# Attention and gated feed-forward on one core: another order inside the planned bursts of a head pair, and the turn of the row maxima as a matmul of its own

## The chip, the core and the metric

The kernel runs on one core of a Trainium2 chip. The metric is the device time of one execution in microseconds, lower is better. The core has a matmul engine (TensorE, "PE" in the profile; "PEld" is its loading of stationary operands), a vector engine (VectorE, "DVE"), an activation engine (ScalarE, "ACT"), a general engine (GpSimd, "POOL"), and SyncE ("SP"), which here only issues transfers. Matmuls write to the PSUM memory, from which only DVE and ACT read here. The kernel cuts PSUM into six single banks (`ps`) and a double one (`pv`). Each engine works through its own list of instructions in order.

## What is computed

Eight batches of eight heads, 576 positions, 64 features per head. Scores get a bias from cumulative sums, a causal mask and a softmax; then comes a feed-forward part with a convolution of three taps along the sequence and a sigmoid gate:

```python
scores = scale * np.matmul(q, k.transpose(0, 1, 3, 2))
cum = np.cumsum(np.maximum(s, 0.0), axis=-1)
bias = -(cum[:, :, :, None] - cum[:, :, None, :])
scores = np.where(causal, -1000000000.0, scores + np.minimum(bias, 0.0))
scores = scores - np.max(scores, axis=-1, keepdims=True)
attn = np.exp(scores)
attn = attn / (np.sum(attn, axis=-1, keepdims=True) + 1e-09)
x = np.matmul(attn, v)          # heads of a batch side by side: 512 features
h = np.maximum(x @ w_in, 0.0)   # 1024 features
conv_out = sum(conv_w[k] * hp[:, k:k + S, :] for k in range(3))
out = (h * (1.0 / (1.0 + np.exp(-conv_out)))) @ w_out
```

## The kernel before

**Pairs.** The 64 heads are worked on as 32 pairs, the two heads of a pair on the two halves of the partitions; four pairs make a batch. For each pair p the function `pair` lays down these steps, named as in the profile by their lines:

- Loads: q and k (L662), values (L667), rows for the bias (L688). Each number of q and k is split into a rounded part (L674) and a rest (L678, POOL).
- *Maxima parts* sh0 to sh3 (L719, PE): rough scores with queries on the partitions, from the rounded parts and the bias rows, two passes each. A part has two PSUM banks, one for each head of the pair. Parts 0 and 1 have 288 columns, parts 2 and 3 have 512 in two pieces each. DVE takes the maximum of each piece (L734) into a column of the tile `r8` and so frees the banks. `r8` has ten columns, five row tiles for each of two heads.
- *The turn* tn (L750, PE): the ten columns of maxima are transposed into rows in a PSUM bank; ACT copies them (L757), and SP moves them by two transfers into the tile `eq` (L763), from where they enter the scores.
- *Scores parts* sc0 to sc3 (L795, PE): the exact scores with keys on the partitions, three passes over q and k and one over bias rows and maxima. Again two banks a part, parts 0 and 1 of 288 columns, parts 2 and 3 of 512. ACT reads them through its exponential-like function (L810) into the tiles `pt` and frees the banks; POOL masks the diagonal blocks (L823).
- *Sums* (L865, PE): row sums of `pt` by a 32-column stationary operand, into one bank. DVE adds a guard and inverts (L884, L885); SP stores the result to memory (L890) and reads it back spread over the partitions (L899).
- *Values* pv (L847, PE): `pt` times the values, into the one double bank `pv`. DVE multiplies it by the inverse (L907, the step nm), ACT and DVE or POOL split the product for the feed-forward (L921, L925).

**Feed-forward.** For each batch and half of the sequence: `moe_h` makes the eight blocks of hidden features, 12 matmuls each (L956), with ReLU (L968) and center tap (L980) mostly on ACT, the two other taps on DVE (L994), the gate on ACT (L1007), the product on DVE (L1013), and the split into `u` (L1020, L1024). `moe_o` makes the four blocks of the output, 24 matmuls each in four chunks of six (L1050), which ACT or DVE copies (L1063) and SP stores. These matmuls use the full 128*128 array; sums use 128*32, values 128*64, scores and maxima 64*128, as the profile shows behind each operation.

**The plan.** Nothing is emitted in the order of the Python loops. Each step is a task with an engine, an estimated cost, the tasks it needs, a due time (tag) and the buffers it takes. `Sched.play` runs them through a simple model of the five engines and emits every engine's list in the order found. For PE it takes the ready task with the lowest tag, where a task in the same array mode as the one before counts as 8 us earlier (`STAY`). Modes are "r" for scores and maxima, "c32" for sums, "c" for values, and none for the feed-forward.

**Groups.** From pair 8 on (`B0`), matmuls of neighbouring pairs are tied into a group: once PE has begun a group, only tasks of this group (`burst`) are taken until it is finished. Group n holds the turn of pair n, the sums and values of pair n-1, the maxima parts of pair n+1 and the scores of pair n. Their order is written out in `ORDER`, and `link` makes it binding: each member follows the one before, and what the members need (handed over by `note`) must be done before the first of them:

```python
ORDER = ("tn", "sum", "pv", "sh0", "sh1", "sc0", "sh2", "sc1", "sh3", "sc2", "sc3")
for t, needs in seq:
    for d in needs:
        sch.need(d, first)
for (a, _), (c, _) in zip(seq, seq[1:]):
    sch.follow(a, c)
```

So the due time of the first member decides when a group competes with the feed-forward. The turn of pair p is due at `a_sh + 1` with `a_sh = at(p-1) + 0.05`, where `at` advances 20.5 us a pair; a maxima part of pair p+1, which stands in the same group, is due at `at(p) + 0.05`. Buffers around the change: `r8`, `rt` and `s` two of each, `ek` and `eq` three, `pt` three (two for a pair), `pv` and `rb` one, PSUM banks six.

Of the kernel before, what the change touches and what calls it, by code (L numbers as in the profile page):

```python
# [11 lines left out]
F32 = mybir.dt.float32  # L12
# [21 lines left out]
STAY = 8.0  # L34

B0 = 8
ORDER = ("tn", "sum", "pv", "sh0", "sh1", "sc0", "sh2", "sc1", "sh3", "sc2", "sc3")

# [39 lines left out]
class Sched:  # L80
# [4 lines left out]
    def add(self, name, opts, deps, tag, emit, alloc=(), uses=(), mode=None, nbytes=0, prev=None,  # L85
            burst=None):

        t = Task()
        t.name, t.opts, t.tag, t.emit = name, opts, tag, emit
        t.alloc, t.uses, t.mode, t.nbytes = alloc, list(alloc) + list(uses), mode, nbytes  # L90
        t.succ, t.start, t.seq, t.eng, t.done = [], None, len(self.tasks), None, None
        for b in t.uses:
            b.users += 1
        t.wait = 0
        for d in deps:
            if d is not None:
                d.succ.append(t)
                t.wait += 1
        t.then, t.burst = [], burst
        if burst is not None:  # L100
            self.size[burst] += 1
        if prev is not None:
            self.follow(prev, t)
        self.tasks.append(t)
        return t
# [142 lines left out]
def kernel(  # L248
# [10 lines left out]
    nc = tc.nc  # L259
    NP, P, _, S = qk.shape  # L260
# [11 lines left out]
    NT = (S + P - 1) // P  # L272
# [7 lines left out]
    const = ctx.enter_context(tc.tile_pool(name="const", bufs=1))  # L280
# [10 lines left out]
    ident = const.tile([P, P], F32, name="ident")  # L291
# [17 lines left out]
    PT_t = [const.tile([P, O_T[-1] + W_T[-1]], F32, name=f"pt{i}") for i in range(NPT)]  # L309
    X_t = const.tile([P, sum(NX), 2, XW], F32R, name="x")  # L310
    rb_t = const.tile([P, S], F32, name="rb")
    R8_t = [const.tile([P, 2 * NT], F32, name=f"r{i}") for i in range(2)]
    RT_t = [const.tile([2 * NT, P], F32R, name=f"rt{i}") for i in range(2)]
    rs_t = const.tile([P, RS], F32, name="rs")
    ri_t = const.tile([P, RS], F32, name="ri")
# [36 lines left out]
    def buf(name, n=1):  # L352
        return Buf(pools[name], n)

    def psb():
        return Buf(pool_ps)

    def bank(b, c0, c1):
        return ps_t[b.slot][:, c0:c1]
# [4 lines left out]
    def c_tt(n):  # L364
        return 0.155 + n / 0.96e3
# [4 lines left out]
    def c_pool(n):  # L370
        return 0.19 + n * 2.1e-3
# [21 lines left out]
    def c_ident(e):  # L393
        make_identity(nc, ident)

        nc.gpsimd.memset(mask, 0.0)
        nc.gpsimd.affine_select(
            out=mask[:, S - P : S], in_=mask[:, S - P : S], pattern=[[-1, P]],
            compare_op=ALU.is_ge, fill=NEG, base=0, channel_multiplier=1,
        )  # L400


        for pt in PT_t:
            nc.gpsimd.memset(pt[J_T[NT - 1] : P, O_T[NT - 1] :], 0.0)
        nc.gpsimd.memset(onehot, 0.0)
        for j in range(2):
            nc.gpsimd.memset(onehot[:, j, j : j + 1], 1.0)
# [10 lines left out]
    def c_ind(t):  # L418
# [9 lines left out]
        for i in range(NE)  # L428
    ]
    t_ident = add("ident", [("POOL", 2.5)], [], -189.5, c_ident)  # L430
    t_eb = add("eb", [("ACT", 0.72)], [t_masks], -188, c_ind(EB_t))
    t_ind = [
# [190 lines left out]
    def group(n, _=None):  # L623
        return n if n >= B0 else None

    def note(n, key, t, needs):
        if n >= B0:
            groups[n][key] = t, needs

    def link():  # L630
        for n, g in sorted(groups.items()):
            seq = [g[k] for k in ORDER if k in g]
            inside = {t for t, _ in seq}
# [4 lines left out]
            for (a, _), (c, _) in zip(seq, seq[1:]):  # L638
                sch.follow(a, c)

    last_ek, last_v = [None], [None]


    L = NT - 1
# [5 lines left out]
    def c_rt(n):  # L650

        return n * 0.461e-3

    def pair(p):
# [21 lines left out]
        def lo(e):  # L676
# [5 lines left out]
        t_lo = add(f"lo{p}", [("POOL", c_pool(2 * S), True), ("DVE", c_tt(2 * S), True, 4.0)],  # L682
                   [t_hi], A - 6, lo, uses=[raw, sb])
# [16 lines left out]
        r8, rt = buf("r8"), buf("rt")  # L700
        maxima = []
        t_mm = None
        for i, part in enumerate(SH_PARTS):
            pbs = [psb(), psb()]

            def sh_mm(e, part=part, pbs=pbs):
                o = 0
                for tau, c0, c1 in part:
                    dst = [bank(pb, o, o + c1 - c0) for pb in pbs]
                    qs = slice(P * tau, P * tau + P)  # L710
                    for k in range(2):
# [13 lines left out]
                       uses=[sb, ek], mode="r", prev=None if p - 1 >= B0 else t_mm,  # L725
                       burst=group(p - 1, f"sh{i}"))
            note(p - 1, f"sh{i}", t_mm, [t_hi, t_dr])
            for j in range(2):
                o = 0
                for tau, c0, c1 in part:  # L730
                    def sh_max(e, j=j, tau=tau, c0=c0, c1=c1, o=o, pb=pbs[j]):
# [12 lines left out]
                            sh_max, uses=[pbs[j], r8])  # L744
                    )
                    o += c1 - c0
        tb = psb()

        def turn(e):
            nc.tensor.transpose(bank(tb, 0, P)[0 : 2 * NT, :], R8_t[r8.slot], ident)  # L750

        t_turn = add(f"tn{p}", [("PE", 0.13)], maxima + [t_ident], a_sh + 1, turn, alloc=[tb, rt],
                     uses=[r8], mode="c32", burst=group(p))
        note(p, "tn", t_turn, maxima)

        def rt_cp(e):
            copy_on(e)(RT_t[rt.slot], bank(tb, 0, P)[0 : 2 * NT, :])  # L757
# [3 lines left out]
        def d_shift(e):  # L761
            for j in range(2):
# [6 lines left out]
        t_shift = add(f"ds{p}", [("SP", 1.5)], [t_rt, *t_ind], a_sh + 1, d_shift, alloc=[eq],  # L769
                      uses=[rt], nbytes=30000)  # L770
# [4 lines left out]
        t_sc = None  # L775
        for i, part in enumerate(SC_PARTS):
            pbs = [psb(), psb()]

            def sc_mm(e, part=part, pbs=pbs):
                o = 0  # L780
                for t, c0, c1 in part:
                    i0, cn = P * t + c0, c1 - c0
                    ks = slice(P * t, P * t + P)
                    dst = [bank(pb, o, o + cn) for pb in pbs]
                    st = S_t[sb.slot].rearrange("p a c -> p (a c)")
                    for k in range(4):
                        for j, r in enumerate(lanes):
                            if k < 3:
                                kk, kq = ((2, 3), (0, 3), (2, 1))[k]
                                l = st[r, kk * S + P * t : kk * S + P * t + P]  # L790
                                m = st[r, kq * S + i0 : kq * S + i0 + cn]
                            else:
                                l = EK_t[ek.slot][r, ks]
                                m = EQ_t[eq.slot][r, PAD + i0 : PAD + i0 + cn]
                            nc.tensor.matmul(dst[j], l, m, start=(k == 0), stop=(k == 3))  # L795
                    o += cn

            w = sum(c1 - c0 for _, c0, c1 in part)
            t_sc = add(f"sc{p}.{i}", [("PE", 4 * c_rt(w))], [t_shift, t_lo], A + 0.1 * i,
                       sc_mm, alloc=pbs + (pts if i == 0 else []), uses=[sb, ek, eq], mode="r",  # L800
                       prev=None if p >= B0 else t_sc, burst=group(p))
            note(p, f"sc{i}", t_sc, [t_lo])
            for j in range(2):
                o = 0
                for t, c0, c1 in part:
                    w = c1 - c0

                    def sc_exp(e, j=j, t=t, c0=c0, c1=c1, o=o, pb=pbs[j]):
                        jt = J_T[t]
                        nc.scalar.activation(  # L810
                            PT_t[pts[j].slot][0:jt, O_T[t] + c0 : O_T[t] + c1],
                            bank(pb, o, o + c1 - c0)[0:jt], AF.Sigmoid,
                            bias=bias_sb[0:jt, t, 2 * p + j : 2 * p + j + 1], scale=0.125,
                        )

                    t_exp = add(f"ex{p}.{j}.{t}.{c0}", [("ACT", 0.25 + w / 1.2e3)],
                                [t_sc, t_bias] + (t_bx if p < 2 else []), A + 0.1 * i, sc_exp,
                                uses=[pbs[j], pts[j]])

                    def sc_mask(e, j=j, t=t):  # L820
                        jt, dg = J_T[t], min(P, W_T[t])
                        reg = PT_t[pts[j].slot][0:jt, O_T[t] : O_T[t] + dg]
                        nc.gpsimd.affine_select(  # L823
                            out=reg, in_=reg, pattern=[[1, dg]], compare_op=ALU.is_ge, fill=0.0,
                            base=0, channel_multiplier=-1,
                        )

                    if c0 == 0:
                        t_exp = add(f"mk{p}.{j}.{t}", [("POOL", 0.29, True)], [t_exp],
                                    A + 0.1 * i, sc_mask, uses=[pts[j]])  # L830
                    masks.append((t, t_exp))
                    o += w


        pv, sb_ = buf("pv"), psb()
# [19 lines left out]
        def sums(e):  # L855

            for t in range(NT):
                for j in range(2):
# [17 lines left out]
        t_pv = add(f"pv{p}", [("PE", 2.75)], [t_v] + [m for t, m in masks], tq + 0.1,  # L876
                   pv_mm(range(NT)), alloc=[pv], uses=[vb, *pts], mode="c",
                   prev=None if p + 1 >= B0 else t_sum, burst=group(p + 1))
        note(p + 1, "sum", t_sum, [t_v] + [m for t, m in masks])
        note(p + 1, "pv", t_pv, [])  # L880
        ri, rb = buf("ri"), buf("rb")

        def inverse(e):
# [23 lines left out]
            nc.vector.tensor_tensor(rb_t, pvt[:, PV0 : PV0 + S], rb_t, op=ALU.mult)  # L907

        t_norm = add(f"nm{p}", [("DVE", 0.77)], [t_rb, t_pv], tq, norm, uses=[rb, pv])
        x = [buf("x0"), buf("x1")]  # L910
        x_bufs[p] = x

# [10 lines left out]
        def x_lo(e):  # L923
# [6 lines left out]
                        tq, x_lo, uses=[rb, *x])  # L930
# [144 lines left out]
    for p in range(NP):  # L1075
        pair(p)
# [63 lines left out]
```

## Time and profile before

| | us |
|---|---|
| three executions | 891.0, 898.09, 901.85 |
| median | 898.09 |
| profiled execution | 900.18 |
| its span, first to last instruction | 898.3 |
| mean granted TensorE clock in it | 0.95 |

The profile belongs to one execution. Its rows count from the first instruction. A timeline row gives start, duration, engine, line, operation, what is written and read, and the number of instructions merged; in brackets stands the idle time of the engine before it and what ended it. A group row gives busy time and the mean duration of one in ns, then the idle time of the engine before these instructions, by cause. Matmuls overlap: the duration of one is longer than its distance to the next, so lengths are best taken from start to start.

### The profile page before, as it was taken

How to read it: one execution, taken by the hardware profiler on the slowest of the kernel's cores; microseconds unless marked ns; L12 is line 12 of the kernel's file. 1: busy time of each engine (PE TensorE's matmuls, PEld its weight loads, DVE VectorE, ACT ScalarE, POOL GpSimd, SP SyncE). 2: the span in 40 equal slices, each digit the busy share in tenths (PEclk: the TensorE clock that was granted, in tenths of full speed). 3: DMA queues.
4: the chain of work that ended last, by engine and by line, in shares of the span. 5: the costliest groups of instructions: out<-in, count | busy, mean ns of one | idle time of the engine just before them, and what ended most of it. 6: DMA issues, size and time to landing. Idle time of an engine off the chain costs nothing.

```text
span 898.3 us, 20425 instructions
## 1 busy us (share of the span) xinstructions
PE 816.2 (91%) x7973; PEld 726.2 (81%) x7973; DVE 554.8 (62%) x1400; ACT 432.9 (48%) x958; POOL 328.6 (37%) x484
## 2 busy tenths in 40 slices
PE   2868688888999999999999999999899999999997
PEld 1746567778888889988888879888788888989996
DVE  8676877884757663766648563766537664636441
ACT  3445454644546363635536263635436363645541
POOL 7334444453332343333523343333423243222211
PEclk9988687896999999999999999999999999999998
DMA  6343323322121222122221222122212211110000
GB/s 183 125 122 110 107 84 107 108 78 89 48 82 60 81 65 65 52 81 67 67 66 49 80 66 69 48 80 68 58 57 66 80 41 29 32 47 17 25 28 26
DMA packets 50187, 63.20 MB, mean 70 GB/s; under 512 B 6063, under 2 KB 39151, under 8 KB 50031
## 3 DMA queue, kind: packets, MB, share of 16 engines
q1 hardware_dynamic: 50091, 61.91, 23.0%
q8 instruction: 62, 1.02, 0.5%
q14 instruction: 34, 0.28, 0.1%
HBM read 48.60 MB, written 13.04 MB: 69 GB/s over the span
## 4 chain that ended last, share of the span: by engine, by line
PE 68%; DVE 10%; DMA 9%; issue 2%; SPq 2%; ACT 1%; POOLq 0%; DVEq 0%; ACTq 0%
PE ps L956 23%; PE ps L1050 22%; PE pv L847 8%; PE ps L795 7%; PE ps L865 6%; DMA rb<-ri_d 6%; DVE junk L734 4%; PE ps L719 3%; DMA ri_d<-ri 2%; DVE rb L907 2%; DMA ht<-w_out 1%; SPq L899 1%; DVE ct L994 1%; DVE ri L885 1%; DVE ct L546 0%
## 5 line engine op out<-in xcount | busy, mean ns | idle before, releaser
L810 ACT ACTIVATE pt<-ps,bias_sb 128x288 f32<-128x288 f32 (+4 forms) x384 | 157.2, 480 | 156.7 <-PE ps L795 129.8
L1050 PE MATMUL ps<-u,wo 128*128 128x288 f32 x1536 | 221.4, 301 | 5.9 <-POOL u L1024 2.9
L956 PE MATMUL ps<-x,wi 128*128 128x290 f32 x1536 | 224.4, 304 | 1.1 <-ACT pt L810 1.0
L1050 PEld LDWEIGHTS ps<-u,wo 128*128 128x128 f32 x1536 | 212.3, 192 | 9.1 <-POOL u L1024 4.1
L956 PEld LDWEIGHTS ps<-x,wi 128*128 128x128 f32 x1536 | 215.8, 195 | 3.4 <-ACT pt L810 1.6
L994 DVE SCALAR_TENSOR_TENSOR ct<-ht,cw_sb,ct 128x288 f32<-128x288 f32 (+1 forms) x256 | 143.6, 564 | 101.3 <-ACT ct L980 96.7
L823 POOL TENSOR_SCALAR_AFFINE_SELECT pt<-pt 128x128 f32<-128x128 f32 x320 | 97.4, 321 | 249.1 <-ACT pt L810 241.5
L1024 POOL TENSOR_TENSOR u<-ct,u 128x576 fp32r<-128x576 f32 x64 | 96.5, 1508 | 225.0 <-ACT u L1020 187.3
L734 DVE CUSTOM_DVE_ANT_0 junk<-ps,mask 128x320 bf16<-128x320 f32 (+2 forms) x320 | 137.5, 430 | 61.2 <-PE ps L719 35.8
L795 PE MATMUL ps<-s 64*128 64x288 f32 (+4 forms) x1152 | 141.5, 334 | 29.8 <-DVE r L734 20.2
L795 PEld LDWEIGHTS ps<-s 64*128 64x128 f32 x1152 | 110.5, 204 | 43.6 <-DVE r L734 28.5
L847 PE MATMUL pv<-pt,v 128*64 128x448 f32 (+4 forms) x768 | 95.5, 399 | 0.5 <-DVE rb L907 0.5
L719 PE MATMUL ps<-s 64*128 64x288 f32 (+4 forms) x384 | 81.0, 345 | 14.3 <-DVE r L734 10.2
L968 ACT ACTIVATE ht<-ps 128x289 f32<-128x289 f32 x128 | 52.7, 411 | 76.2 <-PE ps L956 74.8
L847 PEld LDWEIGHTS pv<-pt,v 128*64 128x64 f32 x768 | 51.0, 139 | 43.7 <-issue 31.2
L678 POOL TENSOR_TENSOR s<-raw,s 128x1152 fp32r<-128x1152 f32 x32 | 85.9, 2684 | 0.7 <-ACT s L674 0.7
L1013 DVE TENSOR_TENSOR ct<-ct,ht 128x576 f32<-128x576 f32 x64 | 62.7, 980 | 22.5 <-ACT ct L1007 22.5
L795 PE MATMUL ps<-eq,ek 64*128 64x288 f32 (+4 forms) x384 | 75.6, 322 | 0.0
L719 PEld LDWEIGHTS ps<-s 64*128 64x128 f32 x384 | 50.0, 199 | 29.9 <-DVE r L734 19.6
L980 ACT ACTIVATE ct<-ht,cw_sb 128x288 f32<-128x288 f32 x127 | 68.4, 539 | 5.8
L719 PE MATMUL ps<-ek,eb 64*128 64x288 f32 (+4 forms) x384 | 65.8, 327 | 2.2 <-DMA ek<-bx 2.2
L865 PE MATMUL ps<-pt,onehot 128*32 128x144 f32 (+4 forms) x1792 | 63.0, 276 | 4.3 <-DVE r L734 1.9
(70 smaller groups left out, 662.6 us busy)
## 6 DMA issues: line engine op xcount, KB each, us to landing
raw<-qk SPq DMA_DIRECT2D x32, 576.0 KB
v<-vp SPq DMA_DIRECT2D x32, 320.0 KB
rb<-ri_d SPq DMA_DIRECT2D x64, 144.0 KB
outT<-ob SPq DMA_DIRECT2D x64, 144.0 KB
ht<-w_in SPq DMA_DIRECT2D x16, 256.0 KB
ht<-w_out SPq DMA_DIRECT2D x16, 256.0 KB
ri_d<-ri SPq DMA_DIRECT2D x32, 72.0 KB
rows_d<-bx SPq DMA_DIRECT2D x1, 1215.0 KB
```

The costliest lines, as they stand in the source:

```text
L678: tt_on(e)(st[:, 0:2, :], R_t[raw.slot], st[:, 2:4, :].bitcast(F32), op=ALU.subtract)
L719: nc.tensor.matmul(dst[j], l, m, start=(k == 0), stop=(k == 1))
L734: nc.vector.tensor_tensor_reduce(out=junk[:, 0 : c1 - c0], in0=bank(pb, o, o + c1 - c0), in1=mask[:, S - w + c0 : S - w + c1], scale=1.0, ...
L795: nc.tensor.matmul(dst[j], l, m, start=(k == 0), stop=(k == 3))
L810: nc.scalar.activation(PT_t[pts[j].slot][0:jt, O_T[t] + c0 : O_T[t] + c1], bank(pb, o, o + c1 - c0)[0:jt], AF.Sigmoid, bias=bias_sb[0:jt, ...
L823: nc.gpsimd.affine_select(out=reg, in_=reg, pattern=[[1, dg]], compare_op=ALU.is_ge, fill=0.0, base=0, channel_multiplier=-1,)
L847: nc.tensor.matmul(pvt[j * D : (j + 1) * D, o0 : o0 + c1 - c0], vt[0:jt, t, j * D : (j + 1) * D], PT_t[pts[j].slot][0:jt, O_T[t] + c0 : O_ ...
L865: nc.tensor.matmul(bank(sb_, o0, o0 + b_ - a_)[32 * g : 32 * g + 32], onehot[:, j, :], src[:, a_ - c0 : b_ - c0], start=t == 0 and j == 0, ...
L956: nc.tensor.matmul(bank(hb, 0, XW), l, r, start=(k == 0), stop=(k == len(seq) - 1))
L994: nc.vector.scalar_tensor_tensor(cc[:, lo:hi], h_[:, sh + lo : sh + hi], cw_sb[:, 3 * f + k : 3 * f + k + 1], cc[:, lo:hi], op0=ALU.mult, ...
L1024: tt_on(e)(uu[:, 1], C_t[ct.slot], uu[:, 0].bitcast(F32), op=ALU.subtract)
L1050: nc.tensor.matmul(bank(pb, 0, HS), l, r, start=(fp == 0 and k == 0), stop=(fp == NF // 2 - 1 and k == len(seq) - 1),)
```

## The change

Four things are changed. The order inside a group becomes: maxima parts 0, 1 and 2 of the next pair, then sums and values of the pair before, then scores part 0, maxima part 3 and the other scores. The turn is no member of a group any more and has no array mode: its operand `r8` is widened from ten to 128 columns, zeros behind the ten, and the whole 128x128 tile is transposed, so it counts as one more full-array matmul that the plan places by its own due time. The arrival of the turned maxima (`t_shift`) becomes a need of the scores in their group, so of the group's start. And the start of group p+1 now also needs the normalization (L907) of pair p-1, which empties the double bank `pv`.

```diff
-ORDER = ("tn", "sum", "pv", "sh0", "sh1", "sc0", "sh2", "sc1", "sh3", "sc2", "sc3")
+ORDER = ("sh0", "sh1", "sh2", "sum", "pv", "sc0", "sh3", "sc1", "sc2", "sc3")
...
-    R8_t = [const.tile([P, 2 * NT], F32, name=f"r{i}") for i in range(2)]
+    R8_t = [const.tile([P, P], F32, name=f"r{i}") for i in range(2)]
...
+        for r8 in R8_t:
+            nc.gpsimd.memset(r8, 0.0)
...
-    last_ek, last_v = [None], [None]
+    last_ek, last_v, last_nm = [None], [None], []
...
-            nc.tensor.transpose(bank(tb, 0, P)[0 : 2 * NT, :], R8_t[r8.slot], ident)
+            nc.tensor.transpose(bank(tb, 0, P), R8_t[r8.slot], ident)
 
         t_turn = add(f"tn{p}", [("PE", 0.13)], maxima + [t_ident], a_sh + 1, turn, alloc=[tb, rt],
-                     uses=[r8], mode="c32", burst=group(p))
-        note(p, "tn", t_turn, maxima)
+                     uses=[r8])
...
-            note(p, f"sc{i}", t_sc, [t_lo])
+            note(p, f"sc{i}", t_sc, [t_lo, t_shift])
...
-        note(p + 1, "pv", t_pv, [])
+        note(p + 1, "pv", t_pv, last_nm[:])
...
+        last_nm[:] = [t_norm]
```

## The prediction

> **What bounds the kernel now.** I read the page first, then windows by stage, then the timeline of single bursts. A burst here is the planned run of matmuls of one group: the turn, sums, values, then scores of pair p mixed with the maxima parts of pair p+1.
>
> ```profile
> PE 816.2 (91%) x7973; PEld 726.2 (81%) x7973; DVE 554.8 (62%) x1400; ACT 432.9 (48%) x958; POOL 328.6 (37%) x484
> 118.00:226.32 108.32, 92.69 (x826) 81.22 (x822) 78.69 (x211) 58.40 (x133) 44.54 (x67) 0.84 0.32 95
> 226.32:783.89 557.57, 539.13 (x5493) 482.66 (x5490) 340.59 (x860) 273.64 (x609) 201.87 (x296) 0.99 0.21 62
> sum 266.51, PE 248.07 PEld 192.56 DVE 175.34 ACT 107.72 POOL 63.95; mean PE 11.28 PEld 8.75 DVE 7.97 ACT 4.90 POOL 2.91
> sum 160.77, PE 142.33 PEld 121.84 DVE 118.04 ACT 76.33 POOL 43.52; mean PE 6.47 PEld 5.54 DVE 5.37 ACT 3.47 POOL 1.98
> sum 276.47, PE 276.47 PEld 275.56 DVE 156.65 ACT 155.35 POOL 133.86; mean PE 13.17 PEld 13.12 DVE 7.46 ACT 7.40 POOL 6.37
> ```
>
> In a window's row stand its length and then the busy time of PE, PEld, DVE, ACT and POOL; after them the granted clock. The three sums are: the 22 bursts from 226.32 to 769.30 (266.51/22 = 12.11 us each); in them the stretch from the first maxima part to the burst's end (160.77/22 = 7.31); and the 21 feed-forward stretches between them. In these last PE is busy for all 276.47 us: only fewer PE us help there. What PE loses in the steady part lies in the bursts, in their second half. One burst:
>
> ```profile
> 501.36 0.27 PE L750 MATMUL ps<-ident,r 128*10 128x128 f32 x1
> 501.56 0.40 ACT L1063 COPY ob<-ps 128x288 f32<-128x288 f32 x1 [2.80 <-PE ps L1050]
> 501.56 1.83 PE L865 MATMUL ps<-pt,onehot 128*32 128x144 f32 x56
> 503.31 2.92 PE L847 MATMUL pv<-pt,v 128*64 128x128 f32 x24
> 503.42 0.31 DVE L884 TENSOR_SCALAR rs<-ps 128x144 f32<-128x144 f32 x1 [4.97 <-PE ps L865]
> 503.77 1.05 DVE L885 RECIPROCAL ri<-rs 128x144 f32<-128x144 f32 x1
> 506.17 0.40 PE L719 MATMUL ps<-s 64*128 64x288 f32 x2
> 506.40 0.29 PE L719 MATMUL ps<-ek,eb 64*128 64x288 f32 x2
> 506.53 0.30 PE L719 MATMUL ps<-s 64*128 64x288 f32 x2
> 506.73 0.46 DVE L734 CUSTOM_DVE_ANT_0 junk<-ps,mask 128x288 bf16<-128x288 f32 x1 [1.91 <-PE ps L719]
> 506.80 0.56 PE L795 MATMUL ps<-s 64*128 64x288 f32 x6
> 507.37 0.46 DVE L734 CUSTOM_DVE_ANT_0 junk<-ps,mask 128x288 bf16<-128x288 f32 x1 [0.17 <-PE ps L795]
> 507.98 0.52 DVE L734 CUSTOM_DVE_ANT_0 junk<-ps,mask,r 128x288 bf16<-128x288 f32 x1
> 509.32 0.62 DVE L734 CUSTOM_DVE_ANT_0 junk<-ps,mask 128x448 bf16<-128x448 f32 x1
> 510.27 0.88 PE L795 MATMUL ps<-s 64*128 64x448 f32 x6 [0.28 <-DVE r L734]
> 510.36 0.62 DVE L734 CUSTOM_DVE_ANT_0 junk<-ps,mask 128x448 bf16<-128x448 f32 x1
> 513.14 1.86 PE L1050 MATMUL ps<-u,wo 128*128 128x288 f32 x12
> ```
>
> PE writes the maxima parts into PSUM banks, two a part, of six in all; a bank is free again once DVE has taken its maximum (L734). DVE has stood idle for 4.97 us before L884, with nothing to do beside sums and values; then all maxima come at once, and PE waits for them ("DVE r L734"). In the worst burst a late transfer stands ahead of them in DVE's queue:
>
> ```profile
> 631.10 1.05 DVE L885 RECIPROCAL ri<-rs 128x144 f32<-128x144 f32 x1
> 639.76 0.76 DVE L907 TENSOR_TENSOR rb<-pv,rb 128x576 f32<-128x576 f32 x1 [2.06 <-DMA rb<-ri_d]
> 640.71 0.41 PE L795 MATMUL ps<-s 64*128 64x320 f32 x1 [1.52 <-DVE r L734]
> 337.75:352.27 14.52, 14.52 (x98) 14.47 (x97) 5.07 (x10) 5.53 (x12) 6.08 (x9) 0.88 0.19 64
> 439.07:452.02 12.95, 12.95 (x98) 12.90 (x97) 5.95 (x10) 5.54 (x12) 6.09 (x9) 1.00 0.23 73
> 539.57:554.00 14.43, 14.43 (x97) 14.39 (x97) 4.73 (x10) 5.54 (x12) 6.09 (x9) 0.88 0.19 66
> ```
>
> The last three are the same feed-forward stretch in three batches. After two bursts with long waits the clock fell to 0.88 on the mean, and the stretch took 1.57 and 1.48 us more.
>
> **The change, part by part.** First a burst's PE work without waits. The last burst has no maxima parts and no waits, so it shows the scores alone:
>
> ```profile
> 788.69 0.67 PE L795 MATMUL ps<-s 64*128 64x288 f32 x6
> 789.86 0.77 PE L795 MATMUL ps<-s 64*128 64x448 f32 x6
> 791.04 0.68 PE L795 MATMUL ps<-s 64*128 64x320 f32 x6
> 792.22 1.88 PE L956 MATMUL ps<-x,wi 128*128 128x290 f32 x12
> ```
>
> Four scores parts take 792.22 - 788.69 = 3.53 us, of which parts 2 and 3 take 1.18 each in four passes; a maxima part of as many columns in two passes is estimated at 0.59. Maxima parts 0 and 1 take 506.80 - 506.17 = 0.63. Sum 5.34, against 7.31 measured: 2.0 us of waits a burst.
>
> *The order.* New: maxima 0 to 2 (0.63 + 0.59), sums (503.31 - 501.56 = 1.75), values (506.17 - 503.31 = 2.86), scores with maxima 3 (3.53 + 0.59). The shape 64*128 of scores and maxima is now entered twice, and its first pair takes 0.23 us (506.17 to 506.40) where the next takes 0.13: 0.10 more. Together 10.05 us.
>
> *Waits left in it*, counted from the burst's start: the first maximum begins at 0.56 (506.17 to 506.73); two of part 0 at 0.61 (507.37 to 507.98) and two of part 1 (507.98 to 509.32) end at 3.1; the sums are done then, and L884 with L885 takes 1.4, to 4.6; part 2 at 1.04 a lane (509.32 to 510.36) ends at 6.7. Scores 0 start on PE at 5.9 in banks of parts 0 and 1; scores 1 want part 2's at 7.1, after 6.7. Maxima 3 are taken by about 9.3. L907's transfer came 7.6 us after the reciprocal's end in the worst burst, here 12.2: behind all maxima, so that wait leaves PE's path. It may then hold back feed-forward work on DVE; PE has 13.17 us of stretch, and I take 0.2 for it. Scores 2 wait for ACT's exponentials of scores 0: 0.2, estimated.
>
> *The head.* The three maxima parts need all six banks at once, and the sums one that DVE has already freed. Late next are the last feed-forward banks:
>
> ```profile
> 526.10 0.27 PE L750 MATMUL ps<-ident,r 128*10 128x128 f32 x1
> 527.03 0.40 ACT L968 ACTIVATE ht<-ps 128x289 f32<-128x289 f32 x1
> ```
>
> Here the last bank is read at 527.43, 1.33 us after the burst began; maxima 2 would want it at 0.63: 0.7 of wait. Behind an output stretch there is none: in the burst above L1063 has read the last bank at 501.96, 0.60 after its begin. I take 0.5, between 0 and 1.3. The maxima on DVE push its leftover feed-forward work behind them; that is in the upper end.
>
> *The turn.* It leaves the burst with its 0.20 us (501.36 to 501.56) and comes back among the feed-forward. Its stationary operand grows from 10 to 128 columns. No row shows it there: between 0 (pipelined) and 0.4 (its 0.20 and two shape changes of 0.10); I take 0.20, the row itself. The Trainium skill, TensorEngine Tiling (Array Packing), section Tile-to-Partition Mapping, says that column tiling rules out the fp32 transpose mode; by that a full-width turn could be shorter than the 0.20 of the 10-column one, and the sum would come out up to 4 us lower over 22, an estimate. No run here shows it. ACT's copy and SP's two eq transfers move with the turn, ahead of a stretch of 13.17 us before the scores need them, and so do not wait behind the ri and rb transfers of the next burst: nothing.
>
> *The rest.* The added condition on L907 and on the eq transfer orders the plan and adds no instruction; nothing. A group's first matmul is now a maxima part, due 19.5 us later in the plan than the turn was, so bursts come later against the feed-forward; as PE is full in those stretches, nothing. Two memsets in the setup go to POOL, 37% busy; nothing, or 0.4 if not covered:
>
> ```profile
> masks.py:197 POOL MEMSET ident<- 128x128 f32 x1 | 0.2, 205 | 0.1
> 193.05 0.27 PE L750 MATMUL ps<-ident,r 128*10 128x128 f32 x1
> 214.79 1.57 PE L956 MATMUL ps<-x,wi 128*128 128x290 f32 x5
> 333.00:337.75 4.75, 3.77 (x39) 3.09 (x39) 3.33 (x14) 2.79 (x7) 2.51 (x4) 1.00 0.08 25
> 337.75:341.20 3.45, 3.45 (x17) 3.45 (x17) 1.55 (x5) 2.04 (x6) 3.25 (x8) 0.58 0.06 14
> ```
>
> *The sum.* New burst with turn: 10.05 + 0.2 + 0.2 + 0.5 + 0.2 = 11.15. Gain 12.11 - 11.15 = 0.96, by 22: 21 us. The first burst (193.05 to 214.79, 21.74 us) can give from 0 to 10.6; I take 4, since weight preparation shares its DVE. The two clock falls: 3. That is 28, from the profiled execution's 900.18 (span 898.3 and 1.9 around it; 0.2% above the median of 898.09): 872. The first 193 us are planned anew too: plus or minus 8, half of the 15.6 us that PE idles from 118 to 226.
>
> **The rivals.**
> A, the forecast: 860 to 880.
> B, the waits go altogether: no head wait, the turn hidden, burst 10.45: 1.66 x 22 = 37, and 7 of the first burst, and 3: 853. For it speaks PE's full stretch; against it the read at 527.43.
> C, the wait only moves: the head costs 1.3, not 0.5, in each burst, 18 us, and the first burst gives nothing: 872 + 22 = 894. That is the change not doing what it says. The read at 527.43 speaks for it; the read at 501.96, behind an output stretch, against.
> D, slower: the wait at the head is so long that the clock falls. From 333.00 to 337.75 PE stood still for 0.98 of 4.75 us, and in the next 3.45 us the clock was 0.58, worth 1.5 us as above. If DVE's first maximum comes 2 us late in each burst, behind feed-forward taps, each loses 2 - 0.5 + 1.5 = 3: 872 + 66 = 938; it passes 2% at 2 us a burst. Against it: the 22 bursts idle PE for 18.4 us of 160.77, 0.84 each, and the stretch from 226.32 to 783.89 still ran at 0.99. The Trainium skill, TensorE: Matmul & The Clock Gate, Part 1, says that the clock is halved after an idle window of some 3.4 us; by that D would stop at 872 + 33 = 905, an estimate. This trace differs: it lowers the clock after 0.98 us of scattered waits.
>
> **How the numbers follow.** A 0.45, B 0.13, C 0.32, D 0.08, and 0.02 for a start stage gone wrong between C and D. About 2% is what a measurement of this kernel can tell from no change: faster (below 880) is A and B, 0.58; same is C and the rest, 0.34; slower is D, 0.08. The range from 852 to 898 leaves out half of B, a little of C, and D: 0.18. A's own range is 860 to 880.
>
> **What would show it.** Right: rows L719 ahead of L865 in every burst, bursts of 10.5 to 11.5 us, no PE wait on "DVE r L734" before L795, L907 behind the last L734 of its burst, clock 1.00 from 226 on. Wrong: a wait of over 1 us before the third maxima part or before L865 (C, D), a clock below 1.00 behind bursts (D), feed-forward stretches in which PE waits for POOL or ACT.

## The result, and the profile after

| | us (runs) | ratio to before, 95% interval |
|---|---|---|
| before, in the runs of this comparison | 897.75 (891.0 to 901.85) | |
| changed | 869.45 (868.43 to 873.69) | 0.970 [0.963, 0.977] |
| profiled execution of the changed kernel, and its span | 870.41, 868.7 | |

The changed kernel is 28 us faster; the forecast was 872. In its rows the maxima are L721 on PE and L736 on DVE, the turn L752, scores L796, values L848, sums L866, L907 has become L908, the taps L996, the feed-forward L958 and L1052.

First the page's busy times of the changed kernel:

```profile
PE 789.9 (91%) x7973; PEld 713.4 (82%) x7973; DVE 558.2 (64%) x1421; ACT 422.4 (49%) x944; POOL 324.9 (37%) x479
```

Then its windows, with columns as in the prediction (length, then busy time of PE, PEld, DVE, ACT, POOL, then granted clock, DMA share, GB/s). The first sum is that of 22 bursts from 224.62 to 756.20, the second that of 20 of the 21 feed-forward stretches between them, without the first.

```profile
226.32:783.89 557.57, 544.98 (x5742) 499.57 (x5743) 360.04 (x896) 276.70 (x624) 199.02 (x298) 1.00 0.21 64
sum 236.88, PE 227.61 PEld 188.79 DVE 180.51 ACT 90.88 POOL 47.58; mean PE 10.35 PEld 8.58 DVE 8.21 ACT 4.13 POOL 2.16
224.62:239.09 14.47, 12.37 (x153) 9.57 (x153) 9.48 (x30) 4.75 (x10) 3.71 (x6) 0.88 0.16 49
sum 268.66, PE 264.43 PEld 259.48 DVE 156.50 ACT 158.08 POOL 136.71; mean PE 13.22 PEld 12.97 DVE 7.82 ACT 7.90 POOL 6.84
```

The granted clock over the steady part reads 1.00 (0.99 before). The one fall that is left lies in the first of the 22 bursts, which takes 14.47 us at 0.88; the other 21 take (236.88 - 14.47) / 21 = 10.59. Before, the same count gives (266.51 - 11.39) / 21 = 12.15, its first burst taking 11.39. The feed-forward stretches, in which PE was never idle before, now hold 268.66 - 264.43 = 4.2 us of idle time, 0.2 each.

A regular burst in the timeline of the changed kernel (here and below, rows picked from a longer view):

```profile
478.23 0.40 PE L721 MATMUL ps<-s 64*128 64x288 f32 x2
478.80 0.46 DVE L736 CUSTOM_DVE_ANT_0 junk<-ps,mask 128x288 bf16<-128x288 f32 x1 [3.18 <-PE ps L721]
479.58 1.82 PE L866 MATMUL ps<-pt,onehot 128*32 128x144 f32 x56
481.34 2.92 PE L848 MATMUL pv<-pt,v 128*64 128x128 f32 x24
481.39 0.62 DVE L736 CUSTOM_DVE_ANT_0 junk<-ps,mask 128x448 bf16<-128x448 f32 x1 [0.17 <-DVE r L736]
484.19 0.67 PE L796 MATMUL ps<-s 64*128 64x288 f32 x6
484.82 0.31 PE L721 MATMUL ps<-s 64*128 64x320 f32 x2
487.09 0.36 DVE L736 CUSTOM_DVE_ANT_0 junk<-ps,mask 128x192 bf16<-128x192 f32 x1
488.50 0.33 PE L752 MATMUL ps<-ident,r 128*128 128x128 f32 x1
488.59 0.65 PE L1052 MATMUL ps<-u,wo 128*128 128x288 f32 x3
```

The maxima on DVE now run while PE does sums and values (479.58 to 484.19), and PE goes into the scores without a wait. The burst takes 10.27 us, and the turn behind it 0.09. Every fourth burst still has a wait of a microsecond at its head, though before the sums and not before the third maxima part, where the prediction put it:

```profile
454.01 3.29 DVE L996 SCALAR_TENSOR_TENSOR ct<-ht,cw_sb,ct 128x287 f32<-128x287 f32 x4
455.45 0.40 PE L721 MATMUL ps<-s 64*128 64x288 f32 x2
457.22 0.45 DVE L736 CUSTOM_DVE_ANT_0 junk<-ps,mask 128x288 bf16<-128x288 f32 x1
457.82 1.83 PE L866 MATMUL ps<-pt,onehot 128*32 128x144 f32 x56 [0.99 <-DVE r L736]
```

Here DVE is inside a run of feed-forward taps when the burst begins; its first maximum starts 1.77 us after the burst, not 0.57 as above. From a burst's start to its sums the four bursts of a batch take 1.35, 1.78, 1.30 and 2.38 us, again and again.

Where the time went can be counted from 240 us on. Up to there both kernels have done the same work (305 and 306 feed-forward matmuls of 3072, and the same bursts), so the start has given nothing. The table is my own sum over the trace: the time from each matmul's start to the next one's, by kind.

| from 240 us on | before | after |
|---|---|---|
| maxima, turn, scores | 162.0 | 131.0 |
| sums | 40.4 | 40.4 |
| values | 65.6 | 65.6 |
| feed-forward | 386.6 | 388.2 |

The difference, 31.0 - 1.6 = 29.4, is the whole difference of the spans (898.3 - 868.7 = 29.6).

### The profile page after: what moved, and what is told of

It reads as the page before. It is cut to its first block, busy times and chain, and to the rows that moved or that the text cites. A ratio compares the mean times of both kernels' runs of the same rounds, so it can differ in the third digit from the quotient of the medians.

```text
span 868.7 us, 20385 instructions
## 1 busy us (share of the span) xinstructions
PE 789.9 (91%) x7973; PEld 713.4 (82%) x7973; DVE 558.2 (64%) x1421; ACT 422.4 (49%) x944; POOL 324.9 (37%) x479
## 4 chain that ended last, share of the span: by engine, by line
PE 72%; DVE 10%; DMA 6%; issue 4%; ACT 4%; POOL 2%; SPq 1%; POOLq 0%; DVEq 0%; ACTq 0%
PE ps L1052 21%; PE ps L958 20%; PE ps L796 11%; PE pv L848 10%; PE ps L866 7%; DVE ct L996 4%; PE ps L721 3%; DMA rb<-ri_d 3%; DVE junk L736 2%; DVE ct L1015 1%; POOL u L1026 1%; DMA ht<-w_out 1%; ACT ct L1009 1%; DMA ek<-bx 1%; ACT ht L970 1%
## 5 line engine op out<-in xcount | busy, mean ns | idle before, releaser
L1052 PE MATMUL ps<-u,wo 128*128 128x288 f32 x1536 | 220.6, 300 | 8.9 <-POOL u L1026 5.3
L958 PE MATMUL ps<-x,wi 128*128 128x290 f32 x1536 | 219.2, 301 | 3.6 <-ACT ht L970 3.6
L1052 PEld LDWEIGHTS ps<-u,wo 128*128 128x128 f32 x1536 | 210.5, 190 | 12.2 <-POOL u L1026 7.4
L996 DVE SCALAR_TENSOR_TENSOR ct<-ht,cw_sb,ct 128x288 f32<-128x288 f32 (+1 forms) x256 | 161.1, 637 | 87.5 <-ACT ct L982 82.5
L958 PEld LDWEIGHTS ps<-x,wi 128*128 128x128 f32 x1536 | 213.1, 193 | 4.3 <-ACT ht L970 3.8
L824 POOL TENSOR_SCALAR_AFFINE_SELECT pt<-pt 128x128 f32<-128x128 f32 x320 | 106.9, 353 | 247.2 <-ACT pt L811 235.4
L736 DVE CUSTOM_DVE_ANT_0 junk<-ps,mask 128x320 bf16<-128x320 f32 (+2 forms) x320 | 136.0, 425 | 75.7 <-PE ps L721 55.7
L1026 POOL TENSOR_TENSOR u<-ct,u 128x576 fp32r<-128x576 f32 x64 | 92.6, 1446 | 225.0 <-ACT u L1022 192.8
L796 PE MATMUL ps<-s 64*128 64x288 f32 (+4 forms) x1152 | 127.6, 318 | 6.4 <-DVE r L736 5.0
L796 PEld LDWEIGHTS ps<-s 64*128 64x128 f32 x1152 | 107.4, 192 | 14.4 <-DVE r L736 6.9
L848 PE MATMUL pv<-pt,v 128*64 128x448 f32 (+4 forms) x768 | 97.5, 405 | 0.0
L848 PEld LDWEIGHTS pv<-pt,v 128*64 128x64 f32 x768 | 52.2, 143 | 44.3 <-issue 32.3
L866 PE MATMUL ps<-pt,onehot 128*32 128x144 f32 (+4 forms) x1792 | 69.0, 289 | 13.3 <-DVE r L736 9.9
L721 PE MATMUL ps<-s 64*128 64x288 f32 (+4 forms) x384 | 66.3, 325 | 13.2 <-DVE r L736 9.5
L796 PE MATMUL ps<-eq,ek 64*128 64x288 f32 (+4 forms) x384 | 77.8, 306 | 0.0
L866 PEld LDWEIGHTS ps<-pt,onehot 128*32 128x32 f32 x1792 | 60.0, 120 | 20.1 <-issue 6.5
L1015 DVE TENSOR_TENSOR ct<-ct,ht 128x576 f32<-128x576 f32 x64 | 50.4, 787 | 35.1 <-ACT ct L1009 35.1
L721 PE MATMUL ps<-ek,eb 64*128 64x288 f32 (+4 forms) x384 | 58.1, 316 | 4.0 <-DMA ek<-bx 4.0
```

Source lines behind the costliest of these rows:

```text
L721: nc.tensor.matmul(dst[j], l, m, start=(k == 0), stop=(k == 1))
L736: nc.vector.tensor_tensor_reduce(out=junk[:, 0 : c1 - c0], in0=bank(pb, o, o + c1 - c0), in1=mask[:, S - w + c0 : S - w + c1], scale=1.0, ...
L824: nc.gpsimd.affine_select(out=reg, in_=reg, pattern=[[1, dg]], compare_op=ALU.is_ge, fill=0.0, base=0, channel_multiplier=-1,)
L848: nc.tensor.matmul(pvt[j * D : (j + 1) * D, o0 : o0 + c1 - c0], vt[0:jt, t, j * D : (j + 1) * D], PT_t[pts[j].slot][0:jt, O_T[t] + c0 : O_ ...
L866: nc.tensor.matmul(bank(sb_, o0, o0 + b_ - a_)[32 * g : 32 * g + 32], onehot[:, j, :], src[:, a_ - c0 : b_ - c0], start=t == 0 and j == 0, ...
L958: nc.tensor.matmul(bank(hb, 0, XW), l, r, start=(k == 0), stop=(k == len(seq) - 1))
```

## The experiments

Three questions were tried: which part of the change gives the gain; what the waits before consisted of; and whether the later due time of a burst, which the prediction counted as nothing, matters. Each ratio is to the kernel before, run beside it. "Burst" is the mean of the last 22 planned bursts of the profiled execution that hold maxima, each from its first matmul's start to the start of the matmul behind it. (The 11.63 in an expectation below also counts the last burst, which holds no maxima; without it that mean is 11.74.) Experiments built on the kernel before keep its line numbers.

**The turn alone.** The changed kernel with the old order of the other members:

```diff
-ORDER = ("sh0", "sh1", "sh2", "sum", "pv", "sc0", "sh3", "sc1", "sc2", "sc3")
+ORDER = ("sum", "pv", "sh0", "sh1", "sc0", "sh2", "sc1", "sh3", "sc2", "sc3")
```

> The changed kernel with the old order inside the group (sums, values, maxima 0 and 1, scores 0, maxima 2, scores 1, maxima 3, scores 2 and 3); the turn stays outside as a 128x128 matmul, with both added conditions and the later due time. Theory 1 (DVE's maxima, brought forward under sums and values, are what pays): only the turn's 0.20 us against the 0.08 it takes among the feed-forward is saved, 22 x 0.12 = 3 us, so 890 to 900 us, and the second half of a burst stays at 7.0 to 7.5 us. Rival 2 (the turn's leaving, or the later due time of the group, is what pays): 865 to 878 us.

Measured: 913.41, ratio 1.021 [1.017, 1.026], outside both ranges: it gives no gain, it loses. The bursts take 12.37 us without the turn, against 12.11 with it before: the waits for the maxima are all back. The rest is a loss in the first pairs. When the second of the 22 bursts begins, both kernels have done the same 384 feed-forward matmuls, here at 258.52 us, before at 250.73: 7.8 us of the 12.5 by which the profiled spans differ (910.8 and 898.3). In the changed kernel, which has done the same work as the kernel before at 240 us, no such loss shows. Which of the parts that this run keeps makes it (the turn's place, its missing array mode, the two added conditions, the due time) was not tried.

**The order alone.** The kernel before, with only the order changed and the turn still at the head:

```diff
-ORDER = ("tn", "sum", "pv", "sh0", "sh1", "sc0", "sh2", "sc1", "sh3", "sc2", "sc3")
+ORDER = ("tn", "sh0", "sh1", "sh2", "sum", "pv", "sc0", "sh3", "sc1", "sc2", "sc3")
```

> The kernel before with the new order alone: the turn stays first in the group, ten columns wide, then maxima 0 to 2, sums, values and the rest; no other edit. Theory 1: nearly the whole gain, less the turn's 0.12 us and two more changes of the array's shape at 0.10 a burst, 22 x 0.3 = 7 us: 872 to 882 us. Rival 2: no gain, 890 to 905 us.

Measured: 883.13, ratio 0.987 [0.983, 0.991], 1 us outside the range. Only about half the gain. Three of four bursts take 10.55 to 11.09 us with the turn, but one in each batch takes 14.5. Its timeline:

```profile
472.78 0.40 PE L719 MATMUL ps<-s 64*128 64x288 f32 x2
473.46 2.04 DVE L994 SCALAR_TENSOR_TENSOR ct<-ht,cw_sb,ct 128x287 f32<-128x287 f32 x4
475.42 0.75 DVE L1013 TENSOR_TENSOR ct<-ct,ht 128x576 f32<-128x576 f32 x1
476.08 0.45 DVE L734 CUSTOM_DVE_ANT_0 junk<-ps,mask 128x288 bf16<-128x288 f32 x1
476.69 3.22 PE L865 MATMUL ps<-pt,onehot 128*32 128x144 f32 x56 [2.38 <-DVE r L734]
```

And three windows over the same burst:

```profile
475.00:478.30 3.30, 1.61 (x33) 1.59 (x36) 2.87 (x9) 0.91 (x2) 1.35 (x1) 0.78 0.02 6
478.30:481.70 3.40, 3.40 (x41) 2.24 (x37) 2.51 (x9) 0.00 (x0) 0.05 (x1) 0.71 0.00 0
481.70:487.00 5.30, 5.30 (x70) 4.79 (x66) 2.36 (x12) 2.75 (x7) 0.79 (x3) 1.00 0.46 131
```

Taps and the product of the feed-forward stand before the first maximum in DVE's queue. PE waits 2.38 us before the sums, and the clock then falls, so that the same 56 sums take 3.22 us and not 1.83. This is the prediction's rival D, wait and clock both, once a batch.

**Two maxima parts ahead.** The changed kernel with parts 0 and 1 ahead of the sums, part 2 behind the first scores:

```diff
-ORDER = ("sh0", "sh1", "sh2", "sum", "pv", "sc0", "sh3", "sc1", "sc2", "sc3")
+ORDER = ("sh0", "sh1", "sum", "pv", "sc0", "sh2", "sc1", "sh3", "sc2", "sc3")
```

> The changed kernel with two maxima parts ahead of the sums, the third between scores 0 and 1 as before. Theory 1 counted through by rows: no wait at the head (four banks of six), 2.5 us of maxima under sums and values, then PE waits for banks about 0.4 us in the second half: bursts of 10.4 to 10.8 us against 10.77 of the changed kernel, 862 to 871 us. Rival 3 (all three must be ahead, as DVE's remaining 4 us of maxima in 5 us of PE work make PE wait): bursts of 11.3 us or more, 880 us or more.

Measured: 869.19, ratio 0.973 [0.967, 0.979]. The same as with three. The head wait is gone (0.73 us from start to sums in every burst), and part of it comes back among the scores: bursts of 10.35 to 11.33, mean 10.68.

**Shorter maxima.** The kernel before, with maxima over 16 columns of each piece; the other columns are left out:

```diff
-                            out=junk[:, 0 : c1 - c0], in0=bank(pb, o, o + c1 - c0),
-                            in1=mask[:, S - w + c0 : S - w + c1], scale=1.0,
+                            out=junk[:, 0 : 16], in0=bank(pb, o, o + 16),
+                            in1=mask[:, S - w + c0 : S - w + c0 + 16], scale=1.0,
```

> The kernel before, where each maximum on DVE goes over the first 16 columns of its piece alone (the other columns are left out of the maximum; plan and order of all engines stay the same). Theory 1 (PE waits for DVE's maxima): about half of the 6.7 us of maxima a pair goes, PE's waits of 2.0 us a burst fall below 0.8, and the time comes to 855 to 872 us with the order of before. Rival 4 (PE waits in truth for ACT's exponentials, or for the late rb transfer that stands ahead of the maxima on DVE's queue): waits of 1.4 us a burst or more remain, 883 us or more.

Measured: 882.3, ratio 0.986 [0.980, 0.992], above the range of the one theory and below that of the other. A maximum of 0.46 us has become one of 0.16, and bursts still take 11.74. A late transfer now stands where the maxima stood, as the timeline shows:

```profile
347.37 0.76 DVE L907 TENSOR_TENSOR rb<-pv,rb 128x576 f32<-128x576 f32 x1 [2.19 <-DMA rb<-ri_d]
348.05 0.16 DVE L734 CUSTOM_DVE_ANT_0 junk<-ps,mask 128x16 bf16<-128x16 f32 x1
348.27 0.71 PE L795 MATMUL ps<-s 64*128 64x320 f32 x6 [1.14 <-DVE r L734]
```

In that timeline DVE reaches L907 early and then waits for the inverted sums to come back from memory; the maximum that would free PE's bank stands behind it. The view of waits counts both sides (us in total, times, the longest), in the kernel before from 240 to 784 us:

```profile
PE ps L795 <- DVE r L734: 12.7, 29, 1.5
DVE rb L907 <- DMA rb<-ri_d: 12.6, 13, 2.5
```

and in this one from 240 to 764 us:

```profile
DVE rb L907 <- DMA rb<-ri_d: 53.4, 21, 5.2
...
PE ps L795 <- DVE r L734: 14.9, 17, 2.2
```

PE's wait under the name of the maxima has not shrunk (12.7 and 14.9 us); DVE's wait for the transfer has grown from 12.6 to 53.4. So the wait named after the maxima may have two causes, and the next two kernels part them.

**L907 behind the maxima.** The kernel before, in which a pair's maxima must precede the normalization that stood among them:

```diff
+        if p - 2 in nms and p - 1 >= B0:
+            for m in maxima:
+                sch.need(m, nms[p - 2])
...
+        nms[p] = t_norm
```

> The kernel before with one more condition in the plan: from the first group on, the normalization L907 of pair p-2 is placed behind all maxima of pair p on DVE. Nothing is left out. Theory 5 (two causes in a row: the late rb transfer in front of the maxima on DVE's queue, and the maxima themselves): only the first goes, the bursts of 12.3 to 15 us fall to about 11.6, the mean from 12.1 to 11.6, and the clock falls behind them go: 880 to 890 us. If the maxima's own 6.7 us are all: 892 to 900 us. If the late transfer is all: 862 to 872 us.

Measured: 878.97, ratio 0.981 [0.979, 0.984], 1 us below the range of the theory of two causes and outside the other two. So some 18 us of the kernel before hang on L907's place: the wait for the transfer, its own 0.75 us ahead of the maxima, and the falls of the clock that went with them. DVE now takes all the pieces and then L907 (here L910), with no wait for the transfer, as its timeline shows:

```profile
408.66 0.36 DVE L734 CUSTOM_DVE_ANT_0 junk<-ps,mask 128x192 bf16<-128x192 f32 x1
408.95 0.08 DVE L734 DVE_READ_ACCUMULATOR2_ANT r<- 128x1 f32 x1
408.95 0.75 DVE L910 TENSOR_TENSOR rb<-pv,rb 128x576 f32<-128x576 f32 x1
```

The bursts are even, 11.35 to 11.71, and the clock does not fall from 226 to 784 us.

**Both.** The two edits above, short maxima and L907 behind them:

> The run with short maxima (first 16 columns of each piece alone, the rest left out of the maximum) and L907 behind them, both in the old order. Theory 5: with both causes gone PE waits less than 0.6 us a burst, the mean burst is 10.6 to 11.0 us against 11.63 with short maxima alone, 858 to 870 us. If the waits left with short maxima alone were ACT's exponentials: 878 us or more.

Measured: 856.25, ratio 0.956 [0.953, 0.958], 2 us below the range; bursts of 10.74, inside theirs. Taking most of the maxima's time away gives 878.97 - 856.25 = 23 us once the transfer is out of the way. But half of this lies in the first pairs, from which the changed kernel gained nothing. Where the second of the 22 bursts begins, with the same 384 feed-forward matmuls done, the profiled executions can be cut in two:

| us | up to there | behind it |
|---|---|---|
| before | 250.7 | 647.6 |
| L907 behind the maxima | 250.3 | 628.8 |
| shorter maxima | 239.5 | 638.0 |
| both | 238.9 | 615.3 |

The gain in the steady part, 29.4 in the changed kernel, thus meets two waits behind one another in DVE's queue: L907 with its transfer, 647.6 - 628.8 = 19, and the maxima's own time, 628.8 - 615.3 = 13.5 with two thirds of it gone. In the changed kernel both are hidden, less what the head still costs.

**Order and due time.** The kernel before with the new order, and the turn, which heads its group, due as late as the maxima are in the changed kernel:

```diff
-ORDER = ("tn", "sum", "pv", "sh0", "sh1", "sc0", "sh2", "sc1", "sh3", "sc2", "sc3")
+ORDER = ("tn", "sh0", "sh1", "sh2", "sum", "pv", "sc0", "sh3", "sc1", "sc2", "sc3")
...
-        t_turn = add(f"tn{p}", [("PE", 0.13)], maxima + [t_ident], a_sh + 1, turn, alloc=[tb, rt],
+        t_turn = add(f"tn{p}", [("PE", 0.13)], maxima + [t_ident], a_sh + (TP if p >= B0 else 1), turn, alloc=[tb, rt],
```

> The run with the new order alone, the turn still first in its group, but its due time moved from at(p-1) + 1.05 to at(p) + 0.05, the due time that the changed kernel's first member has. Theory 6 (the later due time moves the bursts to a place where DVE is free of feed-forward taps, and so the 2.4 us wait before the sums in every fourth burst and the halved clock behind it go): 866 to 877 us. Rival 7 (what the order alone lacks is the turn's leaving, with its shape changes): 879 to 886 us, with every fourth burst at 14.5 us.

Measured: 863.1, ratio 0.961 [0.957, 0.966]: below the range, and 20 us less than the order alone. All bursts but the first of the 22 (12.46) take 10.44 to 10.62 with the turn.

**An early due time in the changed kernel.** Its maxima, which head the group, due as early as the turn was:

```diff
-                       a_sh + 0.1 * i, sh_mm, alloc=pbs + ([r8] if i == 0 else []),
+                       a_sh + 0.1 * i - (TP - 1 if p - 1 >= B0 else 0), sh_mm, alloc=pbs + ([r8] if i == 0 else []),
```

> The changed kernel with the due time of its first group member set back by 19.5 us, to that of the old turn; nothing else. Theory 6: the wait of over 2 us before the sums comes back in some bursts and with it falls of the clock: 877 to 890 us. Rival 7: 865 to 873 us.

Measured: 885.81, ratio 0.988 [0.986, 0.991], some 16 us above the changed kernel. Bursts take 11.2 to 11.3, and every fourth 12.56. The place of the wait was not the one expected in that fourth burst: it lies before scores 0, not before the sums, and the clock does not fall. The timeline of such a burst shows the taps:

```profile
476.03 0.46 DVE L736 CUSTOM_DVE_ANT_0 junk<-ps,mask 128x288 bf16<-128x288 f32 x1 [2.09 <-PE ps L721]
476.41 2.05 DVE L996 SCALAR_TENSOR_TENSOR ct<-ht,cw_sb,ct 128x287 f32<-128x287 f32 x4
481.95 0.45 DVE L736 CUSTOM_DVE_ANT_0 junk<-ps,mask 128x288 bf16<-128x288 f32 x1
482.46 0.66 PE L796 MATMUL ps<-s 64*128 64x288 f32 x5 [0.80 <-DVE r L736]
```

The burst is started before DVE has finished the feed-forward work that the plan gives lower tags than these maxima. Nearly 6 us lie between two maxima of part 0 (476.03 and 481.95). Whether earlier tags for the maxima on DVE would do as well as the later start was not tried.

**The due time alone**, in the old order:

```diff
-        t_turn = add(f"tn{p}", [("PE", 0.13)], maxima + [t_ident], a_sh + 1, turn, alloc=[tb, rt],
+        t_turn = add(f"tn{p}", [("PE", 0.13)], maxima + [t_ident], a_sh + (TP if p >= B0 else 1), turn, alloc=[tb, rt],
```

> The kernel before, order and turn as they were, with the group's due time moved to at(p) + 0.05 and nothing else. Theory 6 as it stands (a later burst finds DVE free of feed-forward taps, whose due time then lies behind that of the maxima): the old order has its maxima at the burst's end, where they gain little from it; with the late transfer still in front of them 885 to 900 us. Rival 8 (the due time alone is what makes the difference between 895 and 863 us): 862 to 876 us.

Measured: 902.7, ratio 1.006 [1.004, 1.009], 3 us above the nearer range; bursts of 12.46, against 12.11 before. By itself the due time gives nothing: it only protects an order that has maxima at the head.

**Order and due time, two parts ahead.** The edit is against the kernel of order and due time:

```diff
-ORDER = ("tn", "sh0", "sh1", "sh2", "sum", "pv", "sc0", "sh3", "sc1", "sc2", "sc3")
+ORDER = ("tn", "sh0", "sh1", "sum", "pv", "sc0", "sh2", "sc1", "sh3", "sc2", "sc3")
```

> The new order with the turn first in the group, the late due time, and two maxima parts ahead of the sums instead of three. Theory 1: the burst is without waits but for 0.1 to 0.4 us in both, so it is within 0.3 us a burst (7 us) of the run with three ahead: 857 to 870 us. If three are needed: 872 us or more.

Measured: 881.77, ratio 0.984 [0.977, 0.990]; the forecast missed. Regular bursts take 10.7, but once in each of three batches two bursts stand close together: one ends at 464.59, the next begins at 470.32 and takes 15.2 us (timeline):

```profile
468.99 5.48 DVE L994 SCALAR_TENSOR_TENSOR ct<-ht,cw_sb,ct 128x288 f32<-128x288 f32 x4
470.32 0.27 PE L750 MATMUL ps<-ident,r 128*10 128x128 f32 x1
470.63 0.40 PE L719 MATMUL ps<-s 64*128 64x288 f32 x2
474.39 0.44 DVE L734 CUSTOM_DVE_ANT_0 junk<-ps,mask 128x288 bf16<-128x288 f32 x1
478.14 0.67 ACT L1020 CAST u<-ct 128x576 fp32r<-128x576 f32 x1 [2.96 <-DVE ct L1013]
479.27 0.67 PE L795 MATMUL ps<-s 64*128 64x288 f32 x6 [1.46 <-ACT pt L810]
```

It is the taps once more: DVE's first maximum comes 3.8 us behind the first maxima matmul, and ACT, which has to free banks for the scores, waits for DVE's feed-forward work too. So this run says little of two parts against three; why the plan bunches here was not found.

**The changed kernel and the best version once more, side by side.** The second is order and due time, unchanged.

> The changed kernel itself, beside the next one on the same chip: 866 to 873 us.

> The new order with the ten-column turn first in its group and the late due time. If the turn's leaving were worth anything, this would be slower than the changed kernel; theory 6 says that the two do not differ by it, and that this one keeps the bursts of 10.4 to 10.6 us with the turn: 858 to 868 us, 3 to 10 us below the changed kernel.

Measured: 872.0, ratio 0.973 [0.969, 0.977], and 861.93, ratio 0.962 [0.958, 0.965]. The version that leaves the turn in the burst beats the changed kernel by 10 us. The profiled spans differ by 870.4 - 861.0 = 9.4. By the same working as in the table above: maxima, turn and scores from 240 us on, 130.9 - 128.3 = 2.6; 29 feed-forward matmuls more done by 240 us, of 0.14 us each, 4.1; and 2762 feed-forward matmuls of 0.1412 us and not 0.1402 with their waits, 2.8. Of these only the first is the same in the earlier executions of the two kernels (spans of 868.7 and 864.9: 131.0 - 128.4 = 2.6, and 306 against 310 feed-forward matmuls by 240 us). Where the rest of the 10 us lies, and whether the turn or the two added conditions make it, is open.

## Why the prediction held, step by step

*The bound.* That only the second halves of the bursts had PE time to give was right: sums and values did not move by 0.1 us, and maxima, turn and scores gave 31.0. What the prediction called "all maxima come at once, and PE waits for them" holds two causes. It showed the late transfer as "the worst burst" only; with L907 behind the maxima 18 us went by that alone.

*The order.* Without waits the prediction worked out 10.05, with 0.2 for scores 2. Bursts without a head wait measure 10.20. No wait of scores on "DVE r L734" (L736 in the changed kernel) is left from 240 us on.

*The head*, 0.5, between 0 and 1.3: over the 22 bursts the way from the start to the sums is 1.78 us on the mean, against 1.30 without a wait: 0.48. The mean is right (0.40 without the first of the 22), but by luck: the cause is not the one argued. The prediction looked at the last bank to come free by an ACT copy and took the sums' bank as free already; PE waits for just that bank, because DVE is still at feed-forward taps. This costs 1.1 us in every fourth burst and 0.5 in another of the four.

*The turn*, 0.20: mis-sized. It costs 0.09 behind a burst (488.50 to 488.59), and less between two feed-forward matmuls (timeline of the changed kernel, like the two fences below):

```profile
205.95 0.96 PE L1052 MATMUL ps<-u,wo 128*128 128x288 f32 x6
206.75 0.27 PE L752 MATMUL ps<-ident,r 128*128 128x128 f32 x1
206.78 0.91 PE L1052 MATMUL ps<-u,wo 128*128 128x288 f32 x5
```

The row that the prediction took was that of the ten-column turn in another array shape; between its ends, 0 and 0.4, the pipelined one was nearer. The Trainium skill, TensorEngine Tiling (Array Packing), section Tile-to-Partition Mapping, says that column tiling excludes the fp32 transpose mode. The direction agrees with these rows; whether that mode is the cause no run here shows, since shape and width were changed together.

*Feed-forward held back by L907*, 0.2 a burst: right, 4.2 us over 20 stretches, in seven waits. One such place, where L908's wait for the transfer passes through the split into `u` to PE:

```profile
514.88 0.76 DVE L908 TENSOR_TENSOR rb<-pv,rb 128x576 f32<-128x576 f32 x1 [2.94 <-DMA rb<-ri_d]
515.56 0.45 DVE L1022 CAST u<-ct 128x576 fp32r<-128x576 f32 x1
516.07 0.53 PE L1052 MATMUL ps<-u,wo 128*128 128x288 f32 x2 [1.03 <-DVE u L1022]
```

*The burst's sum*, 0.96 of gain in each of 22: a steady one gives 12.15 - 10.59 - 0.08 for the turn - 0.2 in the feed-forward = 1.28, and 21 of them 27 us, where 21 were forecast. *The clock falls*, 3: gone, as said, but for the new one in the first of the 22 bursts. There were three, not two: a third feed-forward stretch before, 643.71 to 657.50, ran at 0.93 and took 13.79 us against 12.95 at full clock. *The first burst*, 4: wrong. It went from 21.74 to 20.39, and the next from 11.39 to 14.47, because feed-forward taps on DVE stand before its maxima, and the clock falls behind the wait (sums of 2.71 us, 1.82 in a regular burst):

```profile
224.86 2.11 DVE L996 SCALAR_TENSOR_TENSOR ct<-ht,cw_sb,ct 128x288 f32<-128x288 f32 x2
226.90 0.44 DVE L736 CUSTOM_DVE_ANT_0 junk<-ps,mask 128x288 bf16<-128x288 f32 x1
227.41 0.47 PE L721 MATMUL ps<-s 64*128 64x448 f32 x2 [2.00 <-DVE r L736]
228.15 2.71 PE L866 MATMUL ps<-pt,onehot 128*32 128x144 f32 x56
```

So 872 was met partly by luck, as two terms missed in opposite directions: bursts 6 too low, the start 4 too high.

*The due time.* "As PE is full in those stretches, nothing" is the step that was wrong in kind. Against the old order it is right (the due time alone: ratio 1.006). In the new order it decides 16 us in the changed kernel and 20 in the other: without it DVE's taps precede the maxima.

*The rivals.* The steady burst, 10.59 with 0.08 for the turn and 0.2 in the feed-forward, 10.87, lies between A's 11.15 and B's 10.45. C, the wait moving to the head, is what an early due time makes, 885.81 and 883.13; D's chain of wait and clock fall was seen once a batch in the order alone. In the changed kernel the first is down to 1.1 us in every fourth burst and 0.5 in another, and the second is there once, in the first of the 22 bursts: a wait of over 1 us before the third maxima part and a clock below 1.00, both named by the prediction as signs of being wrong. A third such sign, feed-forward matmuls that wait for POOL, stands in five of the seven waits above, 3.0 us, behind L908.

## What to carry to other kernels

A wait that the profile puts down to one step can hide what stands before that step in the same engine's queue: before shortening the step, move the other one away and see how much of the wait goes with it. When work is brought to the head of a stage, look at what the engine that must consume it is still doing at that moment; the place in the order and the time at which the stage is started have to be changed together. And a small saving that looks free (here a turn of 0.2 us taken out of the burst) should be run by itself: with the conditions added for it, but without the new order, it lost 2%.

## What the hardware showed that was not expected

The full-width fp32 turn takes less of PE than that of ten columns: 0.03 us to the next matmul's start between two feed-forward matmuls and 0.09 behind a burst, against 0.20. Its duration in the row does not show this: 270 and 328 ns, against 272. The ten-column turn was followed by a matmul in another array shape, so how much of the difference is its width is open.

In the changed kernel waits of about 1 us before the sums in every fourth burst left the clock full, and one of 2.00 us in the first of the 22 bursts did not: behind it 1.82 us of sums became 2.71. In the order alone it was a wait of 2.38 us, and 1.83 us of sums became 3.22.
